# A new hand-written order of issue, with other engine choices and 154 filler matmuls, in an attention and gated-product kernel

## The chip, the cores and the metric

The kernel runs on one core of one Trainium2 chip. The metric is the device time of one execution in microseconds, median of several runs on the same chip. Five engines work side by side, each through its own queue in order: TensorE (PE; PEld are its weight loads), VectorE (DVE), ScalarE (ACT), GpSimd (POOL) and SyncE (SP), which here only issues DMAs.

## The reference

Inputs are q, k, v of shape (4, 8, 768, 64), a projection of 64 x 6, and three weights w_a, w_b (512 x 1536) and w_out (1536 x 512), all float32. In each of 4 batches and 8 heads:

```python
q_bucket = np.sum((np.einsum('bhsd,dk->bhsk', q, proj) > 0) * powers, axis=-1)
k_bucket = np.sum((np.einsum('bhsd,dk->bhsk', k, proj) > 0) * powers, axis=-1)
mask = q_bucket[:, :, :, None] == k_bucket[:, :, None, :]
scores = np.where(mask, scale * np.matmul(q, k.transpose(0, 1, 3, 2)), -1000000000.0)
attn = softmax of scores over the last axis, with 1e-09 added to the sum
x = np.matmul(attn, v) with the heads of a token side by side: (3072, 512)
out = ((x @ w_a) * (x @ w_b)) @ w_out
```

## The kernel before

**Tiling.** Query rows come in chunks of 256 (3 chunks in each batch), heads in pairs. A tile is one head and 128 query rows against all 768 keys: 192 tiles. For each tile TensorE makes scores (L1156, two operands A and B that carry high and low halves of q and k and the bucket bits), VectorE takes the row maximum (L1170), a width (L1179) and a bias (L1189 or L1195) follow, ScalarE does the exp with its row sum (L1204), the exp is split into an fp16 high part (a cast, L1215 to L1217) and a low part (a subtraction, L1227 on POOL or L1231 on VectorE), both are transposed by one DMA from SP (the tiles a and at), and 18 matmuls make the product with v (L1246, av). The first 16 tiles go another way: six fp32 transposes on TensorE (L1123, et), a copy (L1130, ec) and fp32 matmuls with v (L1137).

**Preparation.** Keys and queries are loaded in fp32, measured (L769, L1054), scaled by a power of two, split into high and low, transposed (by DMA, L926, or on TensorE, L937, for the first ones), and bucketed by small matmuls (L892, L897). The weights come as 512 KB loads (raw_w, raw_wo), their maximum is taken on VectorE (L643) and spread by a matmul (L590), ScalarE scales them (L551), VectorE packs words (L574), and a cast and a subtraction (L662, L670) make two fp16 parts. All 24 raw weight loads and the preparation of batch 0 fall in the first 150 us.

**The second half.** For each chunk of 256 tokens and each of 12 blocks of 128 of the inner width, 24 matmuls make both gated halves (L1397, ab), ScalarE scales one (L1412), VectorE multiplies (L1420), the product is split (L1428 or L1432, and L1440), and 12 matmuls add into the output (L1450, o). At the end one eviction in two halves (L1480 on ScalarE, L1487 on VectorE) and one whole (L1504 or L1510) go out (L1495, L1528).

**What sets the order.** Every piece of work is an operation (`op(engine, duration, function, key, ...)`), numbered in the order in which the program makes them: 3616 in all. Some have alternatives on other engines. Durations and keys are not used when the kernel is issued; a list written out by hand is:

```python
for x in order:
    if x < 0:
        fill(-x)
        continue
    which, at = divmod(x, 10000)
    o = self.ops[at]
    (o.alt[which - 1][2] if which else o.fn)()
```

So 115 is operation 115 on its usual engine, 10115 the same by its first alternative, 20115 by its second, and -18 is 18 filler matmuls (L1587, 256 columns each, of the identity into a PSUM tile that nobody reads). Each engine gets its operations in the order of the list, and waits where one needs something; what stands behind it waits too. Filler matmuls need only the identity.

Operations that the text names, of the first tiles: TensorE 21 and 25 (transposes of key pair 0), 249 (maximum of weight group w0), 296 (of w2), 107, 123, 115, 131, 178 (scores of tiles), 98 (av of a tile, twelve fp32 matmul records), 166 (buckets of key pair 3, behind the DMA transpose 165). ScalarE 324, 329 (L551), 553 (L1054, sum over the second query chunk, behind its load 552 on SP), 110, 126 (L1195, bias), 111, 127, 119 (L1204, exp of the tiles whose scores are 107, 123, 115). VectorE 14 (L773, magnitude of key pair 0; on ScalarE it is L769), 116, 132, 179 (L1170, row maxima of the tiles of 115, 131, 178), 118 (L1189, a bias), 69 (L856, low part of v), 19 and 163 (L987, a copy), 557 (L992, low part of the second query chunk), 246, 248 (maxima of w0), 398 (L574, first packing of w_out).

Of the kernel before, what the change touches and what calls it, by code (L numbers as in the profile page):

```python
# [75 lines left out]
def constants():  # L76
# [28 lines left out]
    4, 7, 13, 5, 6, 2, 1, 0, 41, 56, 55, 54, 53, 267, 10014, 8, 268, 9, 263, 15, 264, 16, 241, 17, 240, 10003, -27,  # L105
    10, 20018, 42, 244, 11, 245, 19, 27, 10060, 43, 145, 12, 20044, 10059, 20, 10058, 46, 382, 21, -3, 10057, 381,
    10022, 61, 62, 47, 63, 64, 269, 23, -5, 72, 10283, 270, 10048, 24, 73, 25, -10, 265, 45, 26, 266, 20068, 271, 272,
    278, 273, 49, -5, 20070, 274, 243, 282, 275, 10254, 50, 242, 51, -17, 277, 284, 52, 315, 247, 10259, 157, 246,
    10028, 65, 248, 279, 249, 83, 10146, 29, -3, 250, 310, 30, 75, 251, 311, 31, 253, 314, 147, -29, 84, 20032, 258,
    76, 10074, 10085, 255, 86, 87, 148, 10077, 34, 256, 10033, 385, 35, 78, 260, 79, 88, 149, 10036, 291, 99, -3, 71,  # L110
    386, 292, 100, 287, 20150, 89, 91, 288, 10158, 257, 80, 92, 90, 81, 101, 93, 316, 94, 383, 95, 159, -6, 20102,
    10330, 160, 317, 103, 96, -6, 252, 152, 97, 387, 276, 153, 261, 104, 10397, 161, 388, 82, 105, 262, 313, 162, 552,
    312, 37, -3, 384, 306, 318, 38, 319, 164, 280, 39, 389, 289, 165, 151, 40, 390, -9, 320, 391, 281, 321, 290, 324,
    107, 392, 294, 154, 553, 322, 108, 123, -3, 10325, 329, 155, 124, 10109, 156, 166, 20066, 110, 98, 293, 111,
    20285, 125, 554, 126, 295, 326, 115, -3, 127, 116, 20555, 396, 357, 296, -5, 297, 809, 117, 286, 131, 10118, 358,
    167, 119, 298, 112, 132, 178, 113, 133, 10169, 10134, 300, 10301, 179, 120, 114, 10163, 121, 557, 135, 128, 69,
    558, 139, 170, 129, 398, 122, 401, 168, 171, 10180, 10402, 305, 136, 10181, 106, 172, 299, 331, 182, 130, 137,
    302, 362, 173, 174, 186, 307, 183, 399, 187, 323, 559, 138, 556, 184, 140, 188, 560, 303, 20189, 403, 175, 561,
    190, 202, 562, 304, 141, 176, 194, 641, 1090, 404, 203, 191, 335, 177, 192, 204, 339, 393, 20308, 10205, 195, 338,
    206, 361, 142, 400, 334, 196, 185, 197, 10143, 198, 144, 210, 360, 309, 810, 199, 211, 218, 200, 212, 193, 10213,  # L120
    219, 214, 405, 220, 207, 811, 327, 10221, 364, 226, 222, 201, 328, 227, 208, 228, 563, 10229, 340, 230, 215, 564,
    20812, 332, 572, 565, 10566, 209, 814, 567, 216, 573, 581, 568, 815, 348, 223, 359, 394, 10574, 569, 217, 582,
    224, 10575, 234, 583, 363, 576, 225, 10353, 570, 336, 577, 10584, 590, 67, 585, 231, 591, 578, 232, 608, 592, 235,
    337, 593, 233, 594, 333, 579, 609, 10586, 365, 599, -2, 610, 10611, 1066, 236, 612, 587, 341, 571, 600, 237, 613,
    366, -5, 238, 20595, 601, 588, 367, 10602, 239, 617, 603, 596, 580, 618, 372, 626, 619, 458, 368, 614, 597, 10604,
    10620, 627, 621, 342, 457, 628, 10605, 615, 10622, 10813, 343, 589, 459, 10629, 10819, 344, 623, 630, 345, 642,
    606, 460, 346, 598, 352, 643, 651, 20631, 465, 644, 461, 624, 354, 645, 1091, 464, 10632, 646, 410, 652, 462, 635,
    660, 466, 20647, 411, 347, 369, 653, 616, 467, 648, 10654, 607, 661, 633, 655, 472, 662, 10663, 656, 349, 678,
    664, 471, 395, 657, 407, 679, 371, 649, 669, 680, 413, 20350, 468, 625, 10681, 10665, 670, 463, 469, 473, 1092,
    682, 351, 671, 406, 474, 634, 412, 672, 479, 683, 658, 636, 10475, 673, 373, 696, 355, 816, 637, 476, 478, 432,  # L130
    10674, 817, 684, 376, 409, 818, 687, 697, 470, 427, 356, 688, 480, 477, 698, 377, 689, 898, 481, 666, 685, 408,
    650, 374, 10690, 489, 414, 10699, 10482, 691, 10675, 488, 700, 667, 10375, 692, 415, 705, 378, 422, 659, 416, 483,
    676, 490, 417, 820, 706, 379, 693, 484, 491, 10701, 821, 436, 380, 421, 686, 707, 495, 10492, 435, 822, 485, 823,
    10708, 694, 434, 709, 496, 10487, 493, 824, 10702, 668, 497, 423, 838, 10710, 703, 677, 10638, 424, 829, 498, 711,
    839, 503, 1093, 840, 425, 10841, 712, 830, 714, 502, 842, 418, 831, 10486, 832, 847, 499, 833, 1095, 494, 431,
    825, 438, 500, 1096, 856, 504, 848, 419, 834, 501, 826, 426, 857, 695, 849, 858, 505, 850, 704, 20859, 827, 10835,
    506, 509, 10843, 428, 851, 510, 639, 860, 1078, 11094, 874, 715, 507, 437, 836, 511, 429, 713, 844, 512, 875,
    1097, 447, 520, 1098, 430, 845, 861, 433, 865, 876, 11067, 439, 716, 519, 866, 877, 10852, 370, 640, 828, 862,
# [1487 lines left out]
```

## Time and profile before

| | us |
|---|---|
| median of 3 runs (lowest, highest) | 884.22 (884.06, 886.03) |
| the profiled execution | 886.4 |
| its span, first to last instruction | 884.6 |
| busy in the span: PE, PEld | 861.5, 657.9 |
| DVE, ACT, POOL | 616.4, 506.7, 470.4 |
| fillers: 144 matmuls, busy | 21.2 |
| mean granted TensorE clock | 0.996 of full |

Busy time of TensorE is the union of pipelined matmuls whose ends are modelled, so a busy TensorE need not be at its peak. A timeline row gives start and length in us, the engine, the line, the operation, the tiles written and read, the count, and in brackets the idle time of that engine ahead of it with what ended it. Rows of neighbouring like instructions are merged.

### The profile page before, as it was taken

Reading aid. Unit: us, or ns where it says so; the run is one execution under the profiler, and the core shown is the slowest. Engines: PE = TensorE matmul, PEld = TensorE weight load, DVE = VectorE, ACT = ScalarE, POOL = GpSimd, SP = SyncE. Lnnn points to the kernel's source line nnn. Section 1 sums busy time; section 2 is a strip of 40 time slices with the busy share of each in tenths; the row PEclk is TensorE's granted clock in tenths of the full one; section 3 lists DMA queues with packets and bytes.
Section 4 is the critical chain, followed back from the end, with each engine's and each line's share of the span. In section 5 each row is a group of like instructions: output and inputs, shape, how many; then the busy total and the mean of one; then the engine's idle time right before and its main releaser. Section 6 shows DMA issues by size and latency. Waiting matters only on the chain.

```text
span 884.6 us, 22994 instructions
## 1 busy us (share of the span) xinstructions
PE 861.5 (97%) x9271; PEld 657.9 (74%) x9271; DVE 616.4 (70%) x1325; ACT 506.7 (57%) x974; POOL 470.4 (53%) x480
## 2 busy tenths in 40 slices
PE   6889999999999999999999999999999999999997
PEld 5678777777777777777777777777777777777875
DVE  6979999887777876877755575867886657553221
ACT  7979999856566665564454446464575453432121
POOL 4668887866774438654364453465356633442111
PEclk9989999999999999999999999999999999999999
DMA  8976999999998889999885876899998966745000
GB/s 324 333 172 206 170 251 212 174 175 215 206 202 165 161 146 194 184 173 194 153 158 100 138 139 126 157 194 161 208 157 153 166 113 124 115 85 96 2 24 24
DMA packets 417130, 142.60 MB, mean 161 GB/s; under 512 B 388608, under 2 KB 409472, under 8 KB 417024
## 3 DMA queue, kind: packets, MB, share of 16 engines
q1 hardware_dynamic: 417024, 141.14, 81.1%
q8 instruction: 72, 1.18, 0.6%
q14 instruction: 34, 0.28, 0.1%
HBM read 37.82 MB, written 6.29 MB: 50 GB/s over the span
## 4 chain that ended last, share of the span: by engine, by line
PE 82%; DVE 4%; DMA 3%; ACT 2%; POOL 1%; issue 1%; SPq 0%; DVEq 0%; ACTq 0%; POOLq 0%
PE ab L1397 39%; PE o L1450 20%; PE s L1156 12%; PE av L1246 9%; DMA at<-a 2%; DVE mx L1170 1%; DMA kTB_k<-nB_k 1%; POOL a L1227 1%; ACT e L1204 1%; DVE wo_y L574 0%; PE av L1137 0%; PE b_k L897 0%; DVE g L1420 0%; PE b_q L897 0%; DVE a L1231 0%
## 5 line engine op out<-in xcount | busy, mean ns | idle before, releaser
L1397 PE MATMUL ab<-xT,wab 128*128 128x256 f16 x3456 | 407.7, 273 | 1.3 <-DVE g L1420 1.3
L1397 PEld LDWEIGHTS <-wab 128*128 128x128 f16 x3456 | 333.3, 98 | 56.7 <-issue 2.1
L1204 ACT ACTIVATE e<-s,bias,width 128x768 f32<-128x768 f32 x192 | 189.9, 990 | 85.3 <-DVE bias L1189 60.5
L1440 POOL TENSOR_TENSOR g<-g,g 128x256 f16<-128x256 f32 x144 | 113.5, 788 | 217.4 <-ACT g L1428 84.5
L1170 DVE TENSOR_REDUCE mx<-s 128x1 f32<-128x768 f32 x192 | 181.7, 951 | 35.6 <-PE s L1156 35.2
L1450 PE MATMUL o<-wo,g 128*128 128x512 f16 x864 | 206.3, 379 | 0.0
L1227 POOL TENSOR_TENSOR a<-e,a 128x768 f16<-128x768 f32 x102 | 171.9, 1691 | 55.9 <-DVE a L1215 23.3
L1412 ACT ACTIVATE a<-ab,wcut 128x256 f32<-128x256 f32 x144 | 68.0, 472 | 173.8 <-PE ab L1397 168.0
L1420 DVE SCALAR_TENSOR_TENSOR g<-ab,wlow,a 128x256 f32<-128x256 f32 x132 | 63.6, 481 | 138.1 <-ACT a L1412 112.3
L1450 PEld LDWEIGHTS <-g 128*128 128x128 f16 x864 | 81.5, 98 | 78.2
L1246 PEld LDWEIGHTS <-at 128*128 128x128 f16 x3168 | 111.1, 98 | 17.2 <-DMA at<-a 2.0
L1246 PE MATMUL av<-vv,at 128*128 128x64 f16 x3168 | 116.0, 193 | 1.2 <-DMA at<-a 1.0
L1156 PE MATMUL s<-kTA_k,qTA_q 128*128 128x384 f16 x384 | 94.5, 328 | 2.0 <-ACT e L1204 1.0
L1156 PE MATMUL s<-kTB_k,qTB_q 128*128 128x384 f16 x384 | 94.5, 328 | 0.0
L1231 DVE TENSOR_TENSOR a<-e,a 128x768 f16<-128x768 f32 x74 | 77.3, 1049 | 5.8 <-ACT a L1216 3.7
L1216 ACT CAST a<-e 128x768 f16<-128x768 f32 x82 | 67.5, 826 | 6.9 <-DMA at<-a 5.5
L1217 POOL CAST a<-e 128x768 f16<-128x768 f32 x48 | 43.0, 897 | 30.7 <-ACT e L1204 18.7
L1156 PEld LDWEIGHTS <-qTB_q 128*128 128x128 f16 x384 | 37.7, 98 | 25.3 <-issue 0.7
L1195 ACT ACTIVATE bias<-mx,width 128x1 f32<-128x1 f32 x76 | 22.1, 291 | 53.3 <-DVE width L1179 36.8
L1179 POOL TENSOR_SCALAR width<-mx,qsig_q 128x1 f32<-128x1 f32 x51 | 21.4, 419 | 54.0 <-DVE mx L1170 52.8
L1156 PEld LDWEIGHTS <-qTA_q 128*128 128x128 f16 x384 | 34.8, 99 | 16.8 <-issue 3.5
L1432 DVE TENSOR_REDUCE g<-g 128x256 f16<-128x256 f32 x78 | 32.2, 413 | 8.0 <-PE o L1450 5.9
(171 smaller groups left out, 830.4 us busy)
## 6 DMA issues: line engine op xcount, KB each, us to landing
rk_k<-in_k_dram SPq DMA_DIRECT2D x16, 384.0 KB, 4.8
rq_q<-in_q_dram SPq DMA_DIRECT2D x12, 512.0 KB, 4.9
vr<-in_v_dram SPq DMA_DIRECT2D x16, 384.0 KB, 4.2
raw_w<-in_moe_w_b_dram SPq DMA_DIRECT2D x12, 512.0 KB, 6.7
raw_w<-in_moe_w_a_dram SPq DMA_DIRECT2D x12, 512.0 KB, 8.5
raw_wo<-in_moe_w_out_dram SPq DMA_DIRECT2D x12, 512.0 KB, 5.2
out_dram<-ob SPq DMA_DIRECT2D x23, 256.0 KB, 2.8
at<-a SPq DMA_TRANSPOSE x176, 4.1
```

The source lines that it names most:

```text
L1156: nc.tensor.matmul(ps.t[:, jj, :HALF], lhsT=x.t[:, uq, :], rhs=y.t[:, h * NT + jj * 3 : h * NT + jj * 3 + 3, :].rearrange("p t x -> p (t x)"),
L1170: lambda: nc.vector.tensor_reduce(out=mx.t[:, u : u + 1], in_=halves(ps.t), axis=AX.XY, op=ALU.max, negate=True),
L1204: lambda: nc.scalar.activation(flat2(e.t), halves(ps.t), AF.Exp, bias=bias.t[:, u : u + 1], scale=width.t[:, u : u + 1], accum_out=sm.t[:, ...
L1216: ("ACT", 0.725, lambda: nc.scalar.copy(out=a2.t[:, 0], in_=e.t), False),
L1227: lambda: nc.gpsimd.tensor_tensor(out=a2.t[:, 1], in0=e.t, in1=a2.t[:, 0], op=ALU.subtract),
L1231: lambda: nc.vector.tensor_tensor(out=a2.t[:, 1], in0=e.t, in1=a2.t[:, 0], op=ALU.subtract), True,
L1246: nc.tensor.matmul(av.t[:, u, :], lhsT=at.t[:, a + kt, :], rhs=w.t[:, h, kt, x, :], start=i == 0, stop=i == 3 * NT - 1,)
L1397: nc.tensor.matmul(pl.t[:, m, :CH], lhsT=wt(m, wi, cc, f), rhs=xt.t[:, cc // 2, xi, cc % 2 * TPC : (cc % 2 + 1) * TPC, :], start=i == 0, s ...
L1412: lambda a=a, pl=pl, gr=gr: nc.scalar.activation(a.t, pl.t[:, 0, :CH], AF.Copy, scale=wcut[:, gr : gr + 1]),
L1420: lambda a=a, g32=g32, pl=pl, cut=cut: nc.vector.scalar_tensor_tensor(out=g32.t, in0=pl.t[:, 1, :CH], scalar=cut, in1=a.t, op0=ALU.mult, o ...
L1440: lambda g=g, g32=g32: nc.gpsimd.tensor_tensor(out=g[1].t, in0=g32.t, in1=g[0].t, op=ALU.subtract),
L1450: nc.tensor.matmul(po.t[:, u, :], lhsT=g[gi].t[:, us], rhs=wo[f // 2].t[:, f % 2, wi * DM : (wi + 1) * DM], start=f % per_q == 0 and i == ...
```

## The change

Only the list ORDER changes. It holds the same 3616 operations, each once. 281 of them run by another alternative: 63 biases, 42 subtractions (24 from VectorE to POOL, 18 the other way), 39 widths, and casts, copies, splits and evictions. VectorE has 1139 operations for 1155, ScalarE 727 for 726, POOL 486 for 471, TensorE 910 and SP 354 as before. Of TensorE's 910 the longest run that keeps its order has 656, of SP's 354 it has 245. The filler matmuls are 154 in 17 groups, where there were 144 in 18. The first 13 lines and the last one, of 191:

```diff
 ORDER = [
-    4, 7, 13, 5, 6, 2, 1, 0, 41, 56, 55, 54, 53, 267, 10014, 8, 268, 9, 263, 15, 264, 16, 241, 17, 240, 10003, -27,
-    10, 20018, 42, 244, 11, 245, 19, 27, 10060, 43, 145, 12, 20044, 10059, 20, 10058, 46, 382, 21, -3, 10057, 381,
-    10022, 61, 62, 47, 63, 64, 269, 23, -5, 72, 10283, 270, 10048, 24, 73, 25, -10, 265, 45, 26, 266, 20068, 271, 272,
-    278, 273, 49, -5, 20070, 274, 243, 282, 275, 10254, 50, 242, 51, -17, 277, 284, 52, 315, 247, 10259, 157, 246,
-    10028, 65, 248, 279, 249, 83, 10146, 29, -3, 250, 310, 30, 75, 251, 311, 31, 253, 314, 147, -29, 84, 20032, 258,
-    76, 10074, 10085, 255, 86, 87, 148, 10077, 34, 256, 10033, 385, 35, 78, 260, 79, 88, 149, 10036, 291, 99, -3, 71,
-    386, 292, 100, 287, 20150, 89, 91, 288, 10158, 257, 80, 92, 90, 81, 101, 93, 316, 94, 383, 95, 159, -6, 20102,
-    10330, 160, 317, 103, 96, -6, 252, 152, 97, 387, 276, 153, 261, 104, 10397, 161, 388, 82, 105, 262, 313, 162, 552,
-    312, 37, -3, 384, 306, 318, 38, 319, 164, 280, 39, 389, 289, 165, 151, 40, 390, -9, 320, 391, 281, 321, 290, 324,
-    107, 392, 294, 154, 553, 322, 108, 123, -3, 10325, 329, 155, 124, 10109, 156, 166, 20066, 110, 98, 293, 111,
-    20285, 125, 554, 126, 295, 326, 115, -3, 127, 116, 20555, 396, 357, 296, -5, 297, 809, 117, 286, 131, 10118, 358,
-    167, 119, 298, 112, 132, 178, 113, 133, 10169, 10134, 300, 10301, 179, 120, 114, 10163, 121, 557, 135, 128, 69,
-    558, 139, 170, 129, 398, 122, 401, 168, 171, 10180, 10402, 305, 136, 10181, 106, 172, 299, 331, 182, 130, 137,
...
-    3601, 3599, 3593, 3603, 3604, 3600, 3605, 3606, 3608, 3607, 3612, 3614, 13610, 3611, 3613, 3615,
+    4, 7, 13, 6, 0, 56, 41, 2, 1, 55, 54, 53, 268, 267, 10003, 14, 263, 264, -5, 15, -12, 240, 16, 241, 17, 245,
+    20018, 244, 42, 8, 27, 9, -8, 5, 20, 145, 10060, 10, 382, 21, -20, 43, 10059, 11, 20044, 10058, 12, 10057, 46,
+    10022, 61, 10019, 157, 62, 47, 63, 64, 23, -6, 269, 72, 20068, 270, 10048, 24, 73, 25, -10, 265, 45, 26, 266,
+    10283, 271, 242, 272, 278, 49, -4, 273, 274, 20070, 243, 282, 50, 247, 51, -10, 277, 284, 52, 246, 10259, 314,
+    381, 248, 249, -4, 279, 10028, 83, 250, 10254, 311, 65, 10146, 251, 29, 75, 310, 30, 31, 315, 253, 147, -24, 84,
+    10074, 20032, 258, 76, 10085, 255, 86, 87, 148, 10077, 287, 34, 256, 88, 71, 78, 386, 35, 89, 385, 10033, 79, 90,
+    260, 10036, 316, 257, 99, 291, 292, 149, 288, 10158, 100, 91, 80, -7, 150, 92, 10330, 81, 252, 93, 317, 10101, 94,
+    20261, 159, 82, 10102, 95, 275, 160, 152, 103, 96, -6, 388, 262, 153, 97, 161, 383, 162, 104, 384, 552, 98, 105,
+    10325, 387, 280, 313, 37, -3, 10397, 312, 306, 38, 389, 318, 164, 39, 319, 390, -9, 40, 289, 151, 165, 320, 391,
+    281, 321, 290, 324, 107, 293, 154, 108, 329, 123, -18, 20066, 322, 109, 294, 110, 276, 553, 155, 392, 10169, 156,
+    124, 10301, 111, 554, 10125, 295, 809, 326, 115, -5, 126, 127, 116, 20555, 396, 296, 166, 117, 297, 20118, 298,
+    131, 20285, 119, 167, 112, 69, 178, 113, 10163, 300, 132, 286, 168, 120, 114, 133, 121, 299, 10134, 179, 135, 128,
+    557, 401, 170, 398, 558, 122, 139, 129, 171, 10180, 305, 10402, 106, 10181, 172, 173, 331, 182, 136, 137, 307,
...
+    3599, 3593, 3603, 3604, 3600, 3605, 3606, 3608, 3607, 3612, 3614, 3613, 3615, 3610, 3611,
 ]
```

In the first 60 us this moves, among others: SP issues the identity (0) and one load of v ahead of the projection (1, 2); the fillers ahead of operation 249 are 10, not 17, and those after 123 are 18, not 3; 329 and 110 stand ahead of 553; 98 stands behind 104 and ahead of 37; 166 stands behind 115 and 296; 69 and 163 stand ahead of 132; 14 and 19 are on VectorE and 118 on POOL. At the end 3613 (a half eviction on VectorE) stands ahead of 3610, which is on ScalarE.

## Rows read from the trace of the kernel before

**Rows 1.** The page's slices: busy tenths of TensorE and its granted clock, 40 slices.
```profile
PE   6889999999999999999999999999999999999997
...
PEclk9989999999999999999999999999999999999999
```

**Rows 2.** Busy time by stages: us from:to, length, PE, PEld, DVE, ACT, POOL, clock, DMA.
```profile
20.00:26.00 6.00, 3.96 (x42) 3.12 (x40) 5.06 (x9) 4.59 (x6) 2.24 (x2) 1.00 1.04 395
46.00:60.00 14.00, 11.41 (x101) 8.56 (x100) 9.22 (x26) 9.00 (x15) 9.54 (x9) 0.76 0.81 180
60.00:155.00 95.00, 91.07 (x986) 73.15 (x985) 91.02 (x194) 90.40 (x150) 77.47 (x56) 1.00 0.98 204
155.00:860.00 705.00, 704.56 (x7685) 535.21 (x7682) 475.37 (x1000) 364.90 (x751) 355.75 (x381) 1.00 0.81 149
```

**Rows 3.** Timeline of TensorE around 50 us (start, length, what, idle before).
```profile
47.24 0.49 PE L1587 MATMUL warm<-ident 128*128 128x256 f16 x3
50.08 0.76 PE L892 MATMUL b_k<-pjk,kTB_k 128*128 128x6 f16 x24 [2.35 <-DMA kTB_k<-nB_k]
50.69 2.67 PE L1137 MATMUL av<-vr,ec 128*128 128x64 f32 x12
53.16 0.85 PE L1156 MATMUL s<-kTA_k,qTA_q 128*128 128x384 f16 x2
...
60.03 1.45 PE L1137 MATMUL av<-vr,ec 128*128 128x64 f32 x12
```

**Rows 4.** Timeline of ScalarE from 45 to 52 us.
```profile
45.19 1.25 ACT L551 ACTIVATE raw_w<-raw_w,wsc 128x1024 f32<-128x1024 f32 x1
48.83 1.06 ACT L1054 ACTIVATE nB_q<-rq_q 128x1024 bf16<-128x1024 f32 x1 [2.39 <-DMA rq_q<-in_q_dram]
...
49.88 1.24 ACT L551 ACTIVATE raw_w<-raw_w,wsc 128x1024 f32<-128x1024 f32 x1
...
51.33 0.99 ACT L1204 ACTIVATE e<-s,bias,width 128x768 f32<-128x768 f32 x1
```

**Rows 5.** Timeline of VectorE from 50 to 64 us.
```profile
50.52 1.22 DVE L574 SCALAR_TENSOR_TENSOR wab<-raw_w 128x1024 int32<-128x1024 int32 x1
54.68 0.96 DVE L1170 TENSOR_REDUCE mx<-s 128x1 f32<-128x768 f32 x1 [2.94 <-PE s L1156]
...
57.78 0.96 DVE L1170 TENSOR_REDUCE mx<-s 128x1 f32<-128x768 f32 x1 [1.04 <-PE s L1156]
...
60.28 1.28 DVE L992 SCALAR_TENSOR_TENSOR nB_q<-rq_q,qsc_q,nB_q 128x1024 f16<-128x1024 f32 x1
...
62.41 2.14 DVE L574 SCALAR_TENSOR_TENSOR wo_y<-raw_wo 128x1024 int32<-128x1024 int32 x1
```

**Rows 6.** Timeline of SP's queue: the issue of the second query chunk's load.
```profile
40.40 1.02 SPq L1044 DMA_DIRECT2D rq_q<-in_q_dram  x1
```

**Rows 7.** Timeline of TensorE from 20 to 25 us.
```profile
20.74 2.02 PE L1587 MATMUL warm<-ident 128*128 128x256 f16 x17
24.80 0.23 PE L590 MATMUL ps_w<-ident,wmx 128*128 128x128 bf16 x1 [2.04 <-DVE wmx L655]
```

**Rows 8.** Groups by line: busy us, mean ns of one, idle before and its releaser.
```profile
L1227 POOL TENSOR_TENSOR a<-e,a 128x768 f16<-128x768 f32 x102 | 171.9, 1691 | 55.9 <-DVE a L1215 23.3 <-ACT a L1216 23.1 <-issue 6.3
...
L1231 DVE TENSOR_TENSOR a<-e,a 128x768 f16<-128x768 f32 x74 | 77.3, 1049 | 5.8 <-ACT a L1216 3.7 <-POOL a L1217 1.9
...
L1215 DVE CAST a<-e 128x768 f16<-128x768 f32 x46 | 27.6, 600 | 9.2 <-DMA at<-a 5.2 <-ACT e L1204 4.0
```

**Rows 9.** Width operations on POOL: all of the line (ns min/median/max), then one.
```profile
L1179 POOL TENSOR_SCALAR width<-mx,qsig_q x51: 294/301/1362, 28.4 to 796.3; 128x1 f32<-128x1 f32 x51
...
60.28 1.36 POOL L1179 TENSOR_SCALAR width<-mx,qsig_q 128x1 f32<-128x1 f32 x1 [4.03 <-DVE mx L1170]
```

**Rows 10.** Timeline of the end, VectorE's whole eviction and the last DMA issue.
```profile
880.45 0.75 DVE L1510 TENSOR_SCALAR ob<-o,osc 128x512 f32<-128x512 f32 x1 [3.33 <-ACT end L1480]
...
881.65 0.38 SPq L1495 DMA_DIRECT2D out_dram<-end  x1
```

354 rows, old and new, of the table ORDER are left out of this document.

## The prediction

> **What bounds the kernel now.** I read the slices of the page first [rows 1]. From the fourth slice on TensorE is busy in nearly every tenth; what it lacks is in the first three slices, where the clock row also shows an 8, and in the last one. A table by stages [rows 2] puts numbers on that: from 155 to 860 us TensorE is busy 704.56 of 705 us, so no order of the same matmuls can win more than 0.44 us there. From 60 to 155 us it is busy 91.07 of 95, with VectorE at 91.02 and ScalarE at 90.40: three engines share the bound. From 46 to 60 us nobody is: TensorE 11.41 of 14 at a mean granted clock of 0.76, VectorE 9.22, ScalarE 9.00. That is the one stretch in which all wait for one another, so I read it row by row, engine by engine.
>
> On TensorE [rows 3]: three fillers end at about 47.6 us, then the bucket matmuls of key pair 3 (op 166) wait 2.35 us for the DMA transpose of that pair. Behind them stand twelve av matmuls of one tile. They take 2.67 us, where the same twelve take 1.45 us from 60.03: the granted clock is at its lower level, 1.2 GHz, after that idle time. Only then, at 53.16, come the scores of tile op 115.
> On ScalarE [rows 4]: it waits 2.39 us, until 48.83, for the load of the second query chunk (op 553), and in order behind it stand the weight scaling op 329 (49.88), and the exp op 111 (51.33).
> On VectorE [rows 5]: its work ends at 51.74 (50.52 + 1.22), and it waits 2.94 us for the scores of op 115, then 1.04 us for those of op 131.
>
> **The change part by part.** All lengths are of the profiled execution (886.4 us, its span 884.6); the median of the runs is 884.22, 2.2 below, and I carry the sum over as a difference.
>
> *A, 46 to 62 us.* ScalarE's order becomes 324, 329, 110, 553, 111. Scaling 329 and bias 110 go into the 2.39 us wait: exp 111 can start at the end of 553, 49.88 instead of 51.33, and end at some 50.9. TensorE's order becomes scores 123, 18 fillers, scores 115, 5 fillers, the w2 maximum, buckets 166, scores 131; the twelve av matmuls of op 98 now run before 41 us. The 18 fillers take some 2 us (17 take 2.02 us in [rows 7]) and end at 49.2; scores 115 start when exp 111 has emptied its PSUM buffer, 50.95. Idle are then 1.7 us instead of 2.35, and the transpose that ended the old wait at 50.08 has landed before 166 needs it. If the clock stays up, four score matmuls take half of what they took at 53.16, about 0.65 us, and the row maximum of 115 starts on VectorE at 51.75, not 54.68: 2.9 us earlier, just as VectorE's former work ends. From there to op 398 (62.41) VectorE needed 62.41 - 54.68 = 7.73 us, of which 1.04 were wait; one bias (0.13) leaves for POOL, so 6.56 remain, and the new list puts the splitting of V (69) and the copy 163 ahead of row maximum 132. Scores 131 end at some 53.5 and are wanted at 54.9; scores 178 follow exp 119, end at 55.1 and are wanted at 56.2. So no wait is left and 398 starts at 51.75 + 6.56 = 58.3: 4.1 us earlier. Bounds: 1.45 (only ScalarE's swap works) to 4.8. I take 4.1, since each wait that goes has its row. What is late next is the landing of the query chunk: ScalarE still waits for it, now 1.3 us instead of 2.39.
>
> *B, the first 46 us.* Two operations of 1.3 us in sum (the magnitude of key pair 0, the copy 19) come to VectorE, where it waits for loads anyway; the loads are the same, in halves swapped, and the identity goes ahead of the rest of the small loads. Fillers before the w0 maximum go from 17 to 10, and TensorE waits there anyhow, 2.04 us until 24.80 [rows 7]. SP issues the query chunk from 40.40 [rows 6], behind the same transpose as before. A gain here ends at the landing at 48.83, so I take 0; bounds -0.7 and +0.5.
>
> *C, 60 to 155 us.* By the choices in the list VectorE gets two casts more (0.60 us each) and one subtraction more (1.05) [rows 8], less three bias and width operations, of some 0.3 us each if they cost what a width costs on POOL [rows 9]: +1.3, and +2.3 without these. VectorE has 4 of 95 us idle there [rows 2], which may hide all or nothing. I take about half, +0.6; bounds 0 and +2.3.
>
> *D, ten more fillers.* 1.1 us at the pace above. They stand in TensorE's idle time ahead of scores that wait for exps: 0; at the lower clock and on the path 2.2.
>
> *E, 155 to 860 us.* In the whole kernel 24 subtractions go from VectorE to POOL and 18 come back: POOL +6 x 1.69 = 10.1 us, VectorE -6 x 1.05 = 6.3 [rows 8]. TensorE hides both, while POOL has 356 of 705 us of work [rows 2]. They are not spread evenly: in the stretch of the list that holds TensorE's work from 200 to 300 us, POOL does 21 subtractions where it did 9, 12 x 1.69 = 20 us more, of which lighter casts give some 4 back. I take +0.2 for tiles that come late; bounds -0.4 and +2.
> Here a rule weighs in. The row shows a width operation on POOL that takes 301 ns in the median and 1362 at most [rows 9]; the long one lies at 60.28, beside a VectorE subtraction with two SBUF inputs from 60.28 to 61.56 [rows 5]. The Trainium skill, SBUF — State Buffer, section "Who interferes with whom", says that a GpSimd instruction that reads SBUF and a VectorE instruction with two SBUF inputs exclude each other for a whole instruction. The trace agrees in this place, with 1.06 us. By that rule POOL's added work would be longer than its mean says; the sum above goes by the means, and the rule's outcome is the third rival.
>
> *F, the end.* Before, the 0.75 us eviction at 880.45 stands ahead of the last half tile on VectorE, whose DMA issues at 881.65 [rows 10]. Now the half tile goes first and the eviction to ScalarE; the last DMA issues about as early but is twice as large. 0; bounds -0.6 and +0.6.
>
> Sum: -4.1 + 0.6 + 0.2 = -3.3 us: some 883.1 for a profiled execution, 884.2 - 3.3 = **880.9** for the median. A measurement of this kernel can tell about 0.3%, 2.65 us: faster is under 881.6, slower over 886.9.
>
> **The rivals.**
> 1. *The load lands later (slower).* Op 553 still stands ahead of exp 111 on ScalarE, and SP still issues this load behind a transpose that waits for VectorE. It took from 40.40 to 48.83 [rows 4, 6]. Each us later takes one from A; at 52.9 A is gone, and past that the whole front moves. Landing at 56 gives 884.2 + 3.1 + 0.8 = 888.1. For it: 8.4 us is already long, and the weight loads ahead come in another order. Against: the same bytes stand ahead of it.
> 2. *The clock falls at the earlier gap.* With seven fillers fewer the idle time before the w0 maximum grows from 2.04 to 2.8 us, more than the 2.35 that came ahead of the fall [rows 3, 7]. The old fall lasted 14 x 0.24 / 0.5 = 6.7 us by its mean clock [rows 2], in which TensorE did 3.4 us less. The same from 25 us on brings key pair 1, and the scores 107 to 115 with it, 3.4 us later, and takes that from A: 884.2 - 0.7 + 0.8 = 884.3. Against: the last maximum of w0 now stands in the order of its loads, and four fillers follow.
> 3. *POOL gets late in the first steady stretch.* Where POOL does 21 subtractions for 9, a tile's chain is 1.69 - 1.05 = 0.64 us longer [rows 8], and an operation held as the one above adds 1.06. It decides where POOL has no idle time left for a few tiles in a row; two such places cost TensorE 2 x 1.06 = 2.1 us: 883.0. Against: POOL is busy half of the time [rows 2].
>
> That the change does not do what it says can hardly be: each operation stands in the list once, with 154 fillers for 144.
>
> **The numbers.** Forecast 0.52 (its own range 878.5 to 882.5), rival 1 0.14, rival 2 0.13, rival 3 0.15, and 0.06 for a front that gains over 5 us (A at 4.8, B at 0.7, E at 0.4: 878.3). Range 878 to 886.5: from the lower bounds over the second and third rival to a part of the first. Faster: three quarters of the forecast, the 0.06 and a little of rival 3, 0.47; slower: rival 1 from a landing at 54.8 on, 0.12; within 0.3%: the rest, 0.41.
>
> **What would show it.** A is right if the clock row has no 8 in the third slice, VectorE's wait for scores of 115 is under 0.5 us, exp 111 starts right behind the query chunk's sum, and the wo0 packing (L574) starts near 58.3. B is right if the query chunk lands at 48.8 +- 1. C and E are right if TensorE is idle at most 5 us from 58 to 155 and at most 1 us from 155 to 860. The prediction is wrong if a second fall of the clock appears before 60 us, if ScalarE waits past 50 us for the query chunk, or if TensorE waits for transposes of the at tiles after 155 us.

## The result and the profile after

The changed kernel takes 895.45 us in the median of four executions (892.14 to 896.0), the kernel before 884.53 (884.06 to 886.03): ratio 1.0113, 95% interval 1.0085 to 1.0140. It is 10.9 us slower, where 3.3 us less was forecast and the range ended at 886.5. The profiled execution is the shortest of the four: 892.14 us, its span 890.1, 5.5 us over the span before.

The page's slices of the changed kernel, TensorE and its granted clock (to [rows 1]): the 8 in the clock row's third slice is gone, while TensorE has an 8 in the third and in the fifth.
```profile
PE   6989899999999999999999999999999999999997
...
PEclk9999999999999999999999999999999999999999
```
Busy time by stages, with the columns of [rows 2]:
```profile
20.00:26.00 6.00, 4.48 (x36) 3.69 (x35) 5.10 (x11) 4.37 (x4) 3.15 (x3) 0.72 1.01 349
46.00:60.00 14.00, 11.07 (x122) 8.55 (x122) 12.96 (x33) 11.67 (x19) 9.93 (x12) 1.00 0.58 111
60.00:155.00 95.00, 88.68 (x948) 70.47 (x948) 90.98 (x185) 87.86 (x150) 76.32 (x54) 1.00 0.99 211
155.00:860.00 705.00, 699.92 (x7656) 531.35 (x7655) 468.10 (x989) 366.41 (x750) 368.65 (x397) 1.00 0.83 149
```
The clock fell from 46 to 60 us before and does not now; it falls from 20 to 26 instead (0.72). There TensorE waits (to [rows 7]):
```profile
21.71 1.87 PE L937 MATMUL t_q_ACT<-ident,marked 128*128 128x128 f16 x16 [1.52 <-DVE marked L911]
```
sixteen matmuls that stand behind four fillers only, and wait because VectorE marks this query chunk later in the new list. From 60 to 155 us TensorE lost 2.4 us of busy time, and from 155 to 860, where it had 0.44 us idle, it now has 5.08.

Where the time went is read by TensorE's own work: for each amount of finished matmuls (counted by their columns, fp32 twice, fillers left out), the time in the trace after less the time in the trace before. At 51.5 us of the kernel before the change is 3.9 us ahead; at 63 us 2.1, at 101 us 2.6 ahead; at 143 us level; at 175 us 1.6 behind, at 396 us 4.3, at 648 us 5.0, at the end 5.5. So at 51.5 us this execution was ahead by about what part A promised; almost half of that was gone at 63 us, all of it at 143, and it ended 5.5 us behind. The other three executions are 3.1 to 3.9 us longer still; the experiments look for the reasons.

TensorE's timeline of the changed kernel around 50 us (to [rows 3]) shows the 18 fillers and the scores of op 115 behind them at 50.51, where 53.16 was. Behind those a new wait: the w2 maximum (L590) needs one of the two PSUM buffers that scores use, and gets it from an exp after 1.53 us.
```profile
47.84 2.13 PE L1587 MATMUL warm<-ident 128*128 128x256 f16 x18
50.51 0.48 PE L1156 MATMUL s<-kTA_k,qTA_q 128*128 128x384 f16 x2 [0.53 <-ACT e L1204]
...
53.39 0.22 PE L590 MATMUL ps_w<-ident,wmx 128*128 128x128 bf16 x1 [1.53 <-ACT e L1204]
```
ScalarE no longer waits for the query chunk (to [rows 4]); the exp of op 111 follows it directly:
```profile
48.35 1.04 ACT L1054 ACTIVATE nB_q<-rq_q 128x1024 bf16<-128x1024 f32 x1
...
49.39 0.97 ACT L1204 ACTIVATE e<-s,bias,width 128x768 f32<-128x768 f32 x1
```
On VectorE (to [rows 5]) the row maximum follows the packing at once, but the splitting of V (op 69, L856), 1.01 us elsewhere, takes 2.72, and the wo0 packing (L574) starts at 60.86.
```profile
51.65 0.95 DVE L1170 TENSOR_REDUCE mx<-s 128x1 f32<-128x768 f32 x1
...
54.53 2.72 DVE L856 SCALAR_TENSOR_TENSOR vv<-vr,vsc,vv 128x768 f16<-128x768 f32 x1
...
60.86 1.22 DVE L574 SCALAR_TENSOR_TENSOR wo_y<-raw_wo 128x1024 int32<-128x1024 int32 x1
```
On POOL at that time:
```profile
54.30 2.13 POOL L670 TENSOR_TENSOR wab<-wab 128x1024 f16<-128x1024 f32 x1
```
VectorE's 69 ends at 57.25, 0.8 us after POOL's instruction and so a little less than its own length: it was held.

Of the groups in [rows 8] the subtractions changed in number and not in length, while a width operation on POOL now takes 541 ns in the mean, with 2297 at most (to [rows 9]):
```profile
L1227 POOL TENSOR_TENSOR a<-e,a 128x768 f16<-128x768 f32 x108 | 181.0, 1679 | 50.1 <-ACT a L1216 25.4 <-DVE a L1215 17.5 <-DMA at<-a 1.6
L1231 DVE TENSOR_TENSOR a<-e,a 128x768 f16<-128x768 f32 x68 | 70.6, 1040 | 4.6 <-ACT a L1216 2.7 <-POOL a L1217 1.7
```
```profile
L1179 POOL TENSOR_SCALAR width<-mx,qsig_q x56: 296/301/2297, 28.6 to 805.0; 128x1 f32<-128x1 f32 x56
```
The end, ScalarE's eviction and the last DMA issue (to [rows 10]):
```profile
886.43 0.69 ACT L1504 ACTIVATE ob<-o,osc 128x512 f32<-128x512 f32 x1 [0.55 <-DVE end L1487]
887.14 0.33 SPq L1528 DMA_DIRECT2D out_dram<-ob  x1
```
The last issue is 5.5 us later than before, as the last matmuls are.

TensorE's waits of the changed kernel from 160 to 880 us (total, times, longest), where the kernel before had one of 0.4 us:
```profile
PE ps_k L460 <- ACT e L1204: 1.5, 1, 1.5
PE ab L1397 <- DVE g L1420: 1.4, 3, 0.9
PE s L1156 <- DVE g L1420: 0.8, 1, 0.8
PE b_k L897 <- DMA kTB_k<-nB_k: 0.5, 1, 0.5
PE o L1450 <- DVE ob L1510: 0.3, 1, 0.3
PE s L1156 <- ACT e L1204: 0.2, 1, 0.2
```

### The profile page after: what moved, and what is told of

Its sections match the earlier page's. It is cut to its first block, busy times and chain, and to the rows that moved or that the text cites. A ratio compares the mean times of both kernels' runs of the same rounds, so it can differ in the third digit from the quotient of the medians.

```text
span 890.1 us, 22998 instructions
## 1 busy us (share of the span) xinstructions
PE 861.0 (97%) x9281; PEld 657.1 (74%) x9281; DVE 613.6 (69%) x1311; ACT 507.1 (57%) x976; POOL 485.6 (55%) x495
## 4 chain that ended last, share of the span: by engine, by line
PE 73%; DVE 12%; DMA 5%; ACT 3%; issue 3%; POOL 3%; SPq 1%; DVEq 0%; POOLq 0%; ACTq 0%
PE ab L1397 36%; PE o L1450 17%; PE s L1156 10%; PE av L1246 8%; DVE mx L1170 3%; DMA at<-a 2%; DVE wmx L643 2%; DMA rq_q<-in_q_dram 1%; DMA raw_w<-in_moe_w_a_dram 1%; POOL a L1227 1%; ACT e L1204 1%; DVE nB_k L992 1%; DVE a L1231 1%; DVE g L1420 1%; DMA kTB_k<-nB_k 1%
## 5 line engine op out<-in xcount | busy, mean ns | idle before, releaser
L1440 POOL TENSOR_TENSOR g<-g,g 128x256 f16<-128x256 f32 x144 | 115.4, 801 | 215.0 <-DVE g L1432 99.8
L1227 POOL TENSOR_TENSOR a<-e,a 128x768 f16<-128x768 f32 x108 | 181.0, 1679 | 50.1 <-ACT a L1216 25.4
L1231 DVE TENSOR_TENSOR a<-e,a 128x768 f16<-128x768 f32 x68 | 70.6, 1040 | 4.6 <-ACT a L1216 2.7
L1179 POOL TENSOR_SCALAR width<-mx,qsig_q 128x1 f32<-128x1 f32 x56 | 30.3, 541 | 41.5 <-DVE mx L1170 40.2
L1217 POOL CAST a<-e 128x768 f16<-128x768 f32 x43 | 37.4, 873 | 18.1 <-ACT e L1204 10.7
L1428 ACT CAST g<-g 128x256 f16<-128x256 f32 x74 | 29.5, 399 | 19.6 <-DVE g L1420 17.6
```

The lines of the kernel that those rows point to most:

```text
L1227: lambda: nc.gpsimd.tensor_tensor(out=a2.t[:, 1], in0=e.t, in1=a2.t[:, 0], op=ALU.subtract),
L1231: lambda: nc.vector.tensor_tensor(out=a2.t[:, 1], in0=e.t, in1=a2.t[:, 0], op=ALU.subtract), True,
L1440: lambda g=g, g32=g32: nc.gpsimd.tensor_tensor(out=g[1].t, in0=g32.t, in1=g[0].t, op=ALU.subtract),
```

## The experiments

Two lists can be joined wherever both have issued nearly the same operations: at the 426th (some 92 us) the two sets are equal, at the 832nd (some 173 us) they differ by one. That cuts the change into front, middle and rest. Each kernel was timed against the kernel before on the same chip.

**The four joins.**
```
f_after92  = changed[:426] + rest of before     r_after92  = before[:426] + rest of changed
f_after173 = changed[:832] + rest of before     r_after173 = before[:832] + rest of changed
```
f_after92: 

> The list of the changed kernel up to its 426th operation (some 92 us, where both lists have issued the same operations), then the rest in the order and on the engines of the kernel before. Theory (the loss is made behind 92 us, by lateness that the new order itself brings there): the gain of the front, 2.1 to 2.8 us at equal TensorE work by the two traces, stays: 884.5 - 2.4 = 882.1, or up to 885.4 if the 3.3 us by which three of four executions of the changed kernel were longer than the profiled one are made in the front. Rival (from 92 to 155 us VectorE sets the pace, so a front that is early only waits longer there): 884.5 within 0.7, TensorE's idle time from 92 to 155 some 2.4 us more than before.

r_after92: 

> The list of the kernel before up to its 426th operation (some 92 us), then the rest in the order and on the engines of the changed kernel. Theory (the loss is made behind 92 us by the new order there): by the traces the changed kernel goes from 2.1 us early at 92 us to 5.5 late at the end, so 884.5 + 7.6 = 892.1; with no fall of the clock at 21 us, so executions within 1 us of each other. Rival (the rest is only ill fitted to a front that is early, its losses come from the meeting of the two): 885 to 887.

f_after173: 

> The changed list up to its 832nd operation (some 173 us), then the kernel before. Theory (losses are local to the places where TensorE waits): front -2.1, 92 to 173 us +3.7, rest 0: 884.5 + 1.6 = 886.1; to 889.4 if the extra 3.3 us of the longer executions are made in the front. Rival (POOL's added subtractions of 200 to 300 us are the cause): 882.5 to 884.5, since that stretch is as before.

r_after173: 

> The kernel before up to its 832nd operation (some 173 us), then the changed list. Theory (losses local): +3.9, the growth of the lag from 173 us to the end in the traces: 888.4, executions within 1 us of each other. Rival (lateness of the middle is carried into the rest, which by itself keeps TensorE full): within 1 us of 884.5.

Measured, before at 885.17: f_after92 890.73 (ratio 1.0063, 1.0050 to 1.0075), r_after92 892.97 (1.0088, 1.0075 to 1.0102), f_after173 894.46 (1.0109, 1.0096 to 1.0122), r_after173 888.28 (1.0038, 1.0025 to 1.0051). So the front costs 5.6 us, the rest 3.1, and the middle 894.46 - 890.73 = 3.7 or 892.97 - 888.28 = 4.7. These add to 12.4 or 13.4 us, where the whole change costs 10.9: they are prices by stage, not a division of the loss. The first theory had the middle and the rest nearly right and the front wrong by 8 us: the profiled execution of the changed kernel was no guide to it.

**The front.** VectorE's timeline of f_after92 from 31 to 36 us (line numbers two higher; columns as in [rows 5]):
```profile
31.08 2.29 DVE L989 COPY marked<-nB_k 128x768 f16<-128x768 f16 x1
33.30 2.18 DVE L576 SCALAR_TENSOR_TENSOR wab<-raw_w 128x1024 int32<-128x1024 int32 x1
```
and POOL's beside it:
```profile
30.27 2.89 POOL L672 TENSOR_TENSOR wab<-wab 128x1024 f16<-128x1024 f32 x1 [1.00 <-ACT wab L664]
33.25 1.16 POOL L567 TENSOR_SCALAR raw_w<-raw_w 128x1024 int32<-128x1024 uint8 x1
```
The same instructions in the profiled execution of the changed kernel, VectorE:
```profile
32.33 0.35 DVE L987 COPY marked<-nB_k 128x768 f16<-128x768 f16 x1
32.60 1.22 DVE L574 SCALAR_TENSOR_TENSOR wab<-raw_w 128x1024 int32<-128x1024 int32 x1
```
and POOL:
```profile
31.70 4.11 POOL L670 TENSOR_TENSOR wab<-wab 128x1024 f16<-128x1024 f32 x1 [1.18 <-ACT wab L662]
```
It is one list with more than one outcome. Either VectorE's ops 33 and 260 wait for POOL's op 257 and the one behind it (2.9 us more), or POOL waits for VectorE. The new list brings this about: it takes op 150 from POOL, so that 257 begins beside 33 and 260. In the first case TensorE waits (f_after92) ahead of the maximum of key pair 3:
```profile
38.22 0.22 PE L462 MATMUL ps_k<-ident,mx_k 128*128 128x128 bf16 x1 [2.49 <-ACT ec L1132]
```
The copy on ScalarE that ends this wait stands behind an instruction that waited 2.21 us for VectorE. By half microseconds the granted clock is low from 39.0 to 42.4 us and again from 56.1 to 59.5, where the w2 maximum has waited 1.53.

after_again: the changed kernel. 

> The changed kernel once more, for the trace of another execution. Three of four executions were 3.1 to 3.9 us longer than the profiled one. Theory (a race between POOL and VectorE near 31 us: where POOL's op 257 begins first, VectorE's 33 and 260 are held for 2.9 us, where VectorE comes first POOL waits): if this execution takes over 894 us, op 33 takes over 2 us and TensorE waits over 2 us for the maximum of key pair 3; if it takes about 892, op 33 takes 0.35. Rival (the spread is the clock alone): op 33 takes 0.35 us in any case, and the granted clock is low for 6.8 us or more.

893.43 us. VectorE:
```profile
30.94 2.29 DVE L987 COPY marked<-nB_k 128x768 f16<-128x768 f16 x1
33.15 1.21 DVE L574 SCALAR_TENSOR_TENSOR wab<-raw_w 128x1024 int32<-128x1024 int32 x1
```
Op 33 is held and 260 is not, TensorE waits 1.46 us, and the clock is low from 39.4 to 42.8 and from 56.4 to 59.8. Both causes of the spread are in this one trace; its time lies between the two that were named, and the two theories are not told apart by it.

f_150:
```diff
-    316, 257, 99, ..., -7, 150, 92,
+    316, 99, ..., 149, 20150, 257, ..., -7, 92,
```


> The front of the changed list up to its 426th operation and the rest of the kernel before, as in f_after92 (890.73), with one step of the front undone: the scaling of key pair 2 (op 150) is on POOL again, and the wab subtraction (op 257, L670) stands behind it on POOL, as in the kernel before. Theory (in f_after92 VectorE is held from 31.1 to 35.5 us, op 33 for 2.29 us instead of 0.35 and op 260 for 2.18 instead of 1.22, because 257 and 330 run on POOL at that time; TensorE then waits 2.65 us at 35.5 for the maximum of key pair 3): op 33 takes 0.35 and 260 1.22 again, that wait is under 0.5 us, and the time is 2.0 to 3.5 us less, some 888. Rival (the front's price is the clock, which falls at the same waits whatever VectorE does): within 1 us of 890.7.

889.80 (1.0052, 1.0039 to 1.0064), 0.9 less, which the two intervals don't tell from nothing: the rival's range. VectorE's op 33 and a bias behind it:
```profile
32.77 0.36 DVE L987 COPY marked<-nB_k 128x768 f16<-128x768 f16 x1
...
40.08 0.21 DVE L1189 TENSOR_SCALAR bias<-mx,width 128x1 f32<-128x1 f32 x1 [2.16 <-POOL width L1179]
```
Op 33 is not held, as the theory says, and TensorE's wait of 2.49 us is gone; but a width now stands behind the two on POOL, VectorE waits 2.16 us for it, and TensorE 1.58 at 40.76. One lateness took the other's place, so the hold near 31 us is real, and what it costs by itself is not shown.

f_fill:
```diff
-    51, ..., 249, ..., 88, ..., 159, ..., 396, 296,
+    -5, 51, ..., -6, 249, ..., -6, 88, ..., -13, 159, ..., 396, -12, 296,
```


> As f_after92 (890.73), with 42 more fillers in front of five waits of TensorE in the front: 5 ahead of the transpose of query chunk 0 (near 20 us), 6 ahead of the w0 maximum, 6 ahead of the transposes of exp 87, 13 ahead of the maximum of key pair 3 (35.5 us), 12 ahead of the w2 maximum (54.1 us). Theory (the held VectorE sets the front's time): the fillers fill waits only; the granted clock stays at 1.00 but the end moves by no more than what the clock cost, -1 to -2 us: some 889.5. Rival (the clock is the price: two falls of 3.4 us, in each of which TensorE does 1.7 us less): -3.4 us, 887.3.

887.39 (1.0028, 1.0018 to 1.0038), 3.3 less: the rival's number. Of the front's 5.6 us that much comes back when TensorE does not idle in five places. That all of it is the clock is not shown: the rival counted both falls as gone, and one, from 46.6 to 50.0 us, is left in the profiled execution, in which op 33 is held as before and op 260 is not.

f_hold:
```diff
-    257, ..., 262, ..., 69, ..., 10163,
+    10257, ..., 10262, ..., 179, 10163, 168, ..., 557, 69,
```


> As f_fill (887.39), with the places undone where VectorE instructions of the front were held while POOL ran: the two wab subtractions 257 and 262 (L670, 2.1 us on POOL) on VectorE, and the marking copy 163 (L987) and the splitting of V (69) behind the row maximum 179, as in the kernel before. Theory (up to some 92 us VectorE sets the pace, and its instructions 33, 152 and 163 took 2.29, 2.35 and 2.30 us instead of 0.35, 1.01 and 0.35, 5.2 us too much, against 2.3 us for the two subtractions that it now does itself): VectorE's busy time up to 92 us falls by some 2.9 us and the time with it, to 884.5. Rival (VectorE's lateness is hidden behind ScalarE's chain of weight scalings): within 1 us of 887.4.

886.38 (1.0016, 1.0004 to 1.0028): 1.0 less than f_fill, and 0.5 less when each is set against the kernel before on its own chip. The intervals overlap, so nothing is shown won, and the rival stands. VectorE's busy time up to the 426th operation fell by 1.2 us, not 2.9: its 152 and 262 are still held for some 0.3 each, and 69 takes 1.91 where it stands now. Of the front 1.9 us stay. The clock does not explain them: three executions of f_hold at a mean granted clock of 0.999 or more took 885.08 in the median, five such of the kernel before 883.28.

a_alone, part A on the kernel before:
```diff
-    82, 105, ..., 154, 553, ..., 123, -3, ..., 166, ..., 98, ..., 115, -3,
+    82, 98, 105, ..., 154, ..., 123, ..., 110, 553, ..., -18, 115, -5, -3, ..., 296, 166,
```


> The kernel before, with part A of the change alone (46 to 62 us): on ScalarE the scaling 329 and the bias 110 ahead of the query chunk 553; on TensorE the av matmuls 98 ahead of 41 us, 18 fillers between scores 123 and 115, the buckets 166 behind the w2 maximum. Theory of the prediction: the wait of 2.35 us and the fall of the clock behind it go; a fall costs 3.1 us in the executions that have it (883.3 without, 886.4 with), the swap on ScalarE gives 1.45 more: 882.0 to 883.7 against 885.1. Rival (before 62 us ScalarE and VectorE are as late as before, and the wait only moves to the w2 maximum, where the changed kernel waits 1.5 us): within 1 us of 885.1.

886.56 (1.0024, 1.0011 to 1.0037): slower by 2.0. Operations 69, 163 and 118 stay as they are in the kernel before. In its profiled execution the clock does not fall until the end, and eight of its twelve executions have a mean clock of 0.999 or more, where five of 23 of the kernel before do; those eight took 886.27 in the median, those five 883.28. So with A the falls are fewer, and it is some 3 us slower at the same clock. At 51.5 us it is 3.8 ahead of the profiled execution before, as worked out in A; but at 57 us it is 2.3 ahead, and r_after173, with the front of the kernel before and an execution in which the clock did not fall, 3.6; at 143 us they are 3.0 and 4.1 ahead. What makes A late there is not shown. Behind 98 us TensorE's longest waits in a_alone are:
```profile
PE ab L1399 <- DVE g L1422: 2.2, 2, 1.2
PE av L1248 <- DMA at<-a: 2.0, 2, 1.8
PE ps_k L462 <- ACT nB_k L771: 1.8, 2, 0.9
```

b_fill, the clock of the kernel before:
```diff
-    249, ..., 35, ..., 166,
+    -16, 249, ..., -8, 35, ..., -19, 166,
```


> The kernel before with 43 more fillers in front of three waits of TensorE: 16 ahead of the w0 maximum (22.5 us), 8 ahead of the transposes of key pair 1 (29.9 us), 19 ahead of the buckets of key pair 3 (47.5 us); nothing else moved. Theory (its executions take 882.2 to 887 by how often the clock falls behind these waits; without a fall 883.3): 883.0 to 883.6, all executions at a mean granted clock of 1.00. Rival (a fall only uses up time in which TensorE would wait for the exps, or it comes at another wait): within 0.6 us of 884.8.

884.61 against 884.95 (0.9995, 0.9981 to 1.0009): no difference, though 10 of 12 executions had a mean clock of 0.998 or more. Of 35 executions of the kernel before, the 8 at 0.999 or more took 883.95 in the median, the 7 at 0.996 or less 887.0: falls go with up to 3 us, but the median has only 1.0 of that to give. How much of the 3 us is the clock, and how much the lateness that a fall follows, is not told apart. It is the nearest to a better version that the runs found.

**The middle.** m_1080:
```diff
-    872, 926, ..., 454, 1080, 891,
+    872, 1080, 926, ..., 454, 891,
```


> As r_after92 (892.97; the front of the kernel before, the rest of the changed list), with one operation moved on TensorE: the maximum of key pair 1 of block 1 (op 1080, L460) ahead of the scores 926, as in the kernel before, where the changed list has it behind them. Theory (it takes one of the two PSUM buffers that scores use; behind 926 it must wait until the exp of scores 917 is done, 1.7 us near 172): that wait goes, 1.7 us less, 891.3. Rival (the wait moves to scores 926, which then wait for the same buffer, or TensorE's lead is lost at the next tile): within 0.6 us of 892.97.

893.46 (1.0089, 1.0073 to 1.0106): the rival. TensorE waits as long as before, now for the operation's own input:
```profile
172.04 0.23 PE L460 MATMUL ps_k<-ident,mx_k 128*128 128x128 bf16 x1 [1.62 <-DVE mx_k L772]
```
VectorE computes it late, behind a subtraction that took 2.40 us where others take 0.95.

m_casts:
```diff
-    595, ..., 631, ..., 10693, ..., 710,
+    20595, ..., 20631, ..., 693, ..., 10710,
```


> As r_after92 (892.97), with four of its 28 choices from 92 to 173 us undone: the casts 595 and 631 and the subtraction 693 are on POOL and the cast 710 on ScalarE again, as in the kernel before. VectorE loses 0.69 + 0.66 + 0.95 + 1.03 = 3.3 us of work there. Theory (VectorE sets the pace from 92 to 173 us: its operations of that stretch take 76.7 us in r_after92 and 73.3 in r_after173, 3.4 more, and the middle costs 3.7 to 4.7 us): 3.3 us less, 889.7. Rival (POOL or ScalarE is late there, TensorE waits for their results): no gain or a loss, 892.5 to 895.

895.03 (1.0113, 1.0093 to 1.0133): no gain, rather 2 us lost. VectorE gave 3.3 us of work away and its operations of the stretch still keep it busy for 76.4 us (76.7). One of them, VectorE's timeline of m_casts:
```profile
126.70 2.66 DVE L576 SCALAR_TENSOR_TENSOR w_end<-raw_w 128x1024 int32<-128x1024 int32 x1
```
against r_after92:
```profile
124.79 1.22 DVE L576 SCALAR_TENSOR_TENSOR w_end<-raw_w 128x1024 int32<-128x1024 int32 x1
```
with POOL, in m_casts, on the subtraction that came back to it:
```profile
126.34 1.94 POOL L1229 TENSOR_TENSOR a<-e,a 128x768 f16<-128x768 f32 x1 [0.97 <-ACT a L1218]
```
Such holds took 2.3 us of the 3.3.

v_load:
```diff
-    627, 621, ..., 679, 371, ..., 10690, 489, ..., 839, 503, ..., 437, 836,
+    627, -1001, 621, ..., 679, -1001, 371, ..., 10690, -1001, 489, ..., 839, -1001, 503, ..., 437, -1001, 836,
+        if n > 1000: return nc.vector.tensor_reduce(out=junk[:, 0:1], in_=ident.unsqueeze(1).to_broadcast([P, 4, P]), axis=AX.XY, op=ALU.max)
```


> The kernel before with five more reductions on VectorE (128x512 from SBUF, some 0.6 us each, their output unread), one each near 100, 112, 124, 136 and 148 us: 3.0 us of work that nothing waits for. Theory (from 92 to 155 us VectorE sets the pace, nothing added there is hidden): +2.5 to +3.0 us on 884.8. Rival of the prediction (VectorE's 4 idle microseconds between 60 and 155 us hide half): +1.5. Rival (all hidden): under +0.5.

885.83 against 884.95 (1.0010, 0.9995 to 1.0025): 0.9 for 3.0, between "half hidden" and "all hidden". VectorE's sum of work does not set this stretch by itself.

m_order and m_choice:
```
m_order  = before[:426] + changed[426:832] with before's engines + rest of before
m_choice = before, 29 operations of that stretch on changed's engines
```


> The kernel before, with the order of the changed list from its 426th to its 832nd operation (92 to 173 us) and every operation on the engine that it has in the kernel before. The stretch with order and choices costs 3.7 (f_after173 - f_after92) to 4.7 us (r_after92 - r_after173). Theory (the new order costs: operations that TensorE wants early stand behind others on VectorE and POOL): +4 us or more, 889 to 892. Rival (the choices cost, VectorE's 1.5 us of added work and 1.5 us of holds): within 1 us of 884.9.

> The kernel before in its own order, with the 29 choices of engine that the changed list has between 92 and 173 us. Theory (the order costs): +0.5 to +1.5 us, what 1.5 us more on VectorE cost by v_load, and what new holds add: 885.4 to 886.4. Rival (the choices cost): +3 to +4 us, 888 to 889.

Against 885.62: m_order 892.57 (1.0086, 1.0063 to 1.0108), m_choice 887.95 (1.0034, 1.0020 to 1.0048). The order alone costs 7.0 us, the choices alone 2.3, and both together 3.7 to 4.7. So the price of the order depends on the engines that go with it: 7.0 us on the old ones, 1.4 to 2.4 on top of the new choices, which remedy a third to almost a half of it. In m_choice's trace the instructions that it shares with the kernel before on VectorE take 3.1 us longer from 92 to 176 us; that these holds are the choices' price is likely, and not shown.

**The rest.** r_choice:
```
r_choice = r_after173, behind the 832nd operation with before's engines
```


> As r_after173 (888.28; the kernel before up to its 832nd operation, then the changed list), with the order of the changed list but every operation behind the 832nd on the engine that it has in the kernel before (241 choices undone). Theory (POOL's added work, 24 subtractions that came from VectorE against 17 that left, is what makes tiles late): the loss of 3.1 us goes, 885.2 within 0.8. Rival (the order of issue is the cause): 888.3, or more, since the order was made for the other engines.

907.77 (1.0256, 1.0242 to 1.0270): 19.5 more. In this order the new choices as a whole, POOL's added subtractions among them, do not make the rest late; without them it is far worse. What the choices would cost in the old order is not shown.

p_24 and p_48:
```diff
+        if n > 1000: return nc.gpsimd.memset(junk[:, 1:2], 0.0)
```


> The kernel before with 24 tiny memsets on POOL (128x2 floats, some 0.06 us each, unread) between 160 and 400 us, where POOL is idle half of the time. Theory (the 16 KB fetches of instructions, 72 in a run, delay the at transposes in flight by 1.0 us in the median, 4.8 against 3.8 to landing; which transposes they meet depends on how far each engine's instruction stream is): other waits for late transposes behind 160 us, the sum of them 0 to 3 us, unlike before's 0.6. Rival (the fetches don't matter): the same waits at the same operations as before, within 0.4 us of 884.8.

> As p_24 with 48 memsets. Theory: again another set of waits, not twice that of p_24, and it can be less. Rival (the added instructions cost by themselves): twice the difference of p_24.

885.48 (1.0000, 0.9985 to 1.0015) and 885.38 (0.9999, 0.9985 to 1.0014) against 884.95: nothing that can be measured. The sets of waits do differ a little from before's; that this costs is not shown.

What one and the same list loses behind 140 us does vary from trace to trace: against the profiled execution before some 5.7 us more in b_fill, 3.8 in a_alone, 2.3 in f_after92, 0.3 in f_fill, none in f_hold, with not one operation moved there. In b_fill 2.1 us of it are one wait at 205 us, with a fall of the clock behind it from 207.5 to 210.9. What a profiled execution loses in the rest is partly chance; the 3.1 us of r_after173 are a median of six.

## Why the prediction was wrong

Three terms failed: A, put at -4.1, costs 2.0 alone; the rest of the front, B, put at 0, some 3.6 more (5.6 - 2.0, an estimate, since prices by stage do not add exactly); and the order of issue from 60 us on, which had no term, is in the 3.7 to 4.7 us of the middle and the 3.1 of the rest, where C and E put +0.6 and +0.2.

*A, -4.1.* The named rows came as worked out: exp 111 right behind the query chunk, VectorE's wait for the scores of 115 gone, TensorE 3.9 us ahead at 51.5. Two things failed. The sum to op 398 left the held instruction out: 398 came at 60.86, not 58.3, and 1.7 of these 2.6 us are op 69, which the new list sets beside POOL's L670; VectorE's wait of 0.8 for the w2 maximum, which waits for a PSUM buffer, is the rest. Part E of the prediction weighed such holds for POOL alone; the traces show them on both sides, 2.29 us for 0.35 on VectorE and 4.11 for 2.1 on POOL. The Trainium skill, SBUF — State Buffer, section "Who interferes with whom", calls the port pair that the two share an exclusive lock, and says that the order of issue decides who blocks. The traces agree. And the sum took the clock's fall as a fixed property of the kernel before, because the profiled execution had one of 6.8 us. It was carried to a median that, by its executions without a fall, has 1.0 us of it to give. These two say why little was won, not why A alone costs 2.0: a_alone leaves 69 where it was, and the cause of its loss stays open.

*B, 0.* "VectorE waits for loads anyway" covered what came to VectorE, and nothing was worked out for POOL's op 257 being set beside VectorE's 33 and 260. Op 33 was held in four of the five traces with this list, and op 260 in two of them. With the waits and falls of the clock the front costs 5.6 us, of which fillers give 3.3 back; undoing the hold of 33 and 260 alone gave nothing clear, so what the hold costs is argued and not shown.

*C, +0.6.* The middle costs 3.7 to 4.7. The work of the choices was not counted too low (C had +1.3; by the lengths of the same instructions the choices from 92 to 173 us bring VectorE some 0.8 net), and taking half of VectorE's added work as hidden was if anything too dear (0.9 us for 3.0). What failed is that C prices the choices by their work only: the choices alone cost 2.3, and the order of issue has no term in the sum, where it costs 7.0 on the old engines and 1.4 to 2.4 on the new ones. TensorE was idle for 6.3 us from 60 to 155, over the 5 that the prediction allowed from 58 on.

*D, 0.* Not contradicted: 43 more fillers in b_fill cost nothing that can be measured, and 42 more in the new front win 3.3.

*E, +0.2.* The rest costs 3.1, over the bound of 2. The bound came from POOL's load; in r_choice that load is gone, with the other choices, and the time rises. TensorE's idle time, 5.08 us for "at most 1", is made of waits of 1.5 us and less for exps, for VectorE's g and for a DMA.

*F, 0.* Right: 5.5 us behind at the last matmuls and at the end.

*Rivals.* The query chunk did not land late (first rival): ScalarE took it up at 48.35. The second was nearest: the clock does fall at earlier gaps, though not ahead of the w0 maximum but of a query transpose (profiled execution) or behind the maximum of key pair 3, and it comes on top of other losses. The third had its stretch wrong: from 200 to 300 us TensorE was idle for 0.5 us where it had been for none, from 300 to 400 for 1.6 where it had been for 0.4. The rows named as signs of failure, a second fall before 60 us and TensorE waiting for transposes, are both in after_again, the second weakly: the at tiles named there cost TensorE 0.2 us behind 155 us, the transposes of key pairs 0.9.

## What to carry to other kernels

An order has a price of its own, which depends on the engines that go with it: cut both lists where they have issued the same operations and time the joins, before summing edits. When an operation is moved to or on POOL, list the VectorE instructions that will run beside it, since either may wait for the whole of the other, and the outcome can change from execution to execution (op 33 took 0.35 us in one execution of the changed kernel and 2.29 in another). A loss seen in one profiled execution, a fall of the clock above all, is worth only what the median of the executions holds of it.

## What was not expected of the hardware

One kernel's executions differ in their falls of the clock: ahead of the end, the two profiled executions of the changed kernel have one of 3.4 us and two of 3.4. The one before has one of 6.8, while six of the 35 executions of that kernel show a mean granted clock of 1.000.

Fetches of instructions meet transposes. The page counts 72 packets of 16 KB in queue q8 in a run, each about 1.0 us long. Of 1584 at transposes in nine traces, the 635 with such a packet in the first 3.5 us after issue landed after 4.7 us in the median, the other 949 after 3.9; 34% of the first took over 5 us, and 13% of the second. In f_after92 one lies beside a transpose that POOL waits for ahead of TensorE's wait of 0.93 us that ends at 533.58; the DMA view from 526 to 530 us (queue: packets, MB, share; then the transpose and its time to landing):
```profile
q8 instruction: 1, 0.02, 2.2%
...
at<-a SPq DMA_TRANSPOSE x1, 5.3
```
That the fetch is what delays the transpose is not shown. Whether moving these fetches could win time stays open: p_24 and p_48 moved POOL's and showed nothing.
